# Moving two start-up dependencies in a fused dynamic-convolution and FFN kernel: when w_out is let in, and when w_in's exchanged copies are made

## The chip, the cores and the metric

The kernel runs on one core of one Trainium2 chip. The metric is the device time of one execution in microseconds (us). A *profile* is one execution under the hardware profiler. Its times count from the first instruction, and its span is some 1.7 us shorter than the device time.

## The reference

```python
def _attn_ref(x, weight_gen):              # x (8, 4096, 192), weight_gen (8, 4096, 8, 7)
    w = softmax(weight_gen, axis=-1)       # over the 7 taps
    x_pad = pad 6 zero rows in front of each sequence
    # out[s, head] = sum over k of w[s, head, k] * x_pad[s + k, head]
def _moe_ref(x, w_in, w_out):              # 32768 tokens, w_in (192, 2048), w_out (2048, 192)
    h = np.maximum(x @ w_in, 0.0)
    return h * h @ w_out
```

## The kernel before

The engines are PE (matrix products; PEld is its weight load), DVE (vector work), ACT (activations and copies), GpSimd (POOL in the profile) and SP, which here only issues DMA transfers. The profile infers from the recorded updates of *semaphores* what ended an engine's wait. For each of GpSimd's row DMAs (below) the trace records 16 such updates, its *landings*. I say that a DMA *lands* when its last update is recorded. The *granted clock* is the share of PE's full clock that the profile shows.

The tokens are worked in blocks: two of 512 tokens (one sub-block each), then blocks of 1024 (two sub-blocks). For the third and fourth blocks, where this change acts, DVE makes the softmax weights in pieces, DMAs of up to 16 KB each move their rows to the partitions where they are needed (`wr`; I call these the *row DMAs*), and DVE multiplies the rows by a mask into *bands* (`bd`). PE convolves x with the bands (`yp`), 16 *units* of h matmuls follow, ACT applies relu (`t`), DVE squares (`g`), and the output matmuls (`o`) come in quarters. I call the bands by sub-block: B2 belongs to the third block, B4 to the fourth.

The parts that the change touches, with cuts marked:

```python
    def cross_w_in(q):            # w_i[:, q, 1] is w_i[:, q, 0] with partition halves exchanged
        for r0, r1 in ((0, RT), (RT, 0)):
            nc.sync.dma_start(out=w_i[r0 : r0 + RT, q, 1], in_=w_i[r1 : r1 + RT, q, 0])
    ...
        x_load_f32(0)
        load_w_in(w_st[0], 0, nc.sync)         # first half of w_in, f32 staging
        load_w_in(w_st[1], 1, nc.sync)         # second half
        ...
        x_load_f32(1)                          # second x load, x_st[1]
        s1.load(nc.sync)
        ...
        nc.gpsimd.tensor_copy(out=gate, in_=x_st[1][:, 0:1])   # the gate
        for q in range(4):
            load_w_out(q, 4)                   # on GpSimd, behind the gate
        s2.load(nc.gpsimd)
        x_load(2)
    ...
        plans = {
            0: "B1 X1 W u u u u E1 C S1 u u M u u",
            1: "L3 u u B2 M E2 B3 u M E2 u u S2 u M u C u S2 M",
            2: "L4 u u u E3 M u u u M B4 u u u u M B5 S3 u u u u M u E3 C u",
            ...
        }
    ...
        for j in range(NBLK):
            if j + 2 < NBLK:
                load_rows(j + 2)
            if 1 <= j <= WQ:                   # WQ = 2
                cross_w_in(j - 1)
            u = 0
            for step in plans[j].split():
                ...
```

In a plan `u` is a unit, `M` a quarter of the output matmuls, `C` the next block's convolution, `B` bands, `E` exponentials, `S` a softmax piece, `W` the cast of w_in's second half, `L` a load of weight_gen, `X` a cast of x. The last piece of a small softmax also issues its row DMAs, in turn from SP and from GpSimd. Units 8 to 15 of a paired block need the second exchanged copy of w_in. The gate copy has no result that anyone uses: it makes GpSimd's stream wait for the tile that it reads (5.88 us of idle time ahead of the copy at 14.56 in before). Its intent is to keep w_out from competing with loads needed earlier.

The softmax here doesn't subtract the row's maximum and nothing guards it: scores larger than these inputs give would overflow.

## Time and profile before

| | before |
|---|---|
| device time, median of 3 runs | 739.93 us (739.14 to 740.39) |
| span in the profile | 737.6 us |
| mean granted PE clock | 0.998 |
| PE waits for w_out, once | 1.73 us |
| PE waits for w_in's second exchanged copy, twice | 2.04 and 0.40 us |

The totals of the profile of before give, for each engine, busy microseconds, share of the span and instructions:

```profile
PE 727.1 (99%) x14053; PEld 528.2 (72%) x14053; DVE 630.1 (85%) x858; ACT 613.3 (83%) x731; POOL 97.7 (13%) x139
```

A kernel at 99% PE can be helped only in the few places where PE idles or runs at a lower clock. The timeline of SP's queue of before (start, duration, queue and line, transfer and count) shows why the second exchanged copy is late:

```profile
27.23 1.85 SPq L142 DMA_DIRECT2D w_i<-w_i  x2
...
34.38 10.16 SPq L352 DMA_DIRECT2D wr<-v_first  x6
44.59 2.26 SPq L142 DMA_DIRECT2D w_i<-w_i  x2
```

SP issued these in program order. The second pair of exchanges stands behind six row DMAs, which wait for a softmax piece that ends at 41.33 and are all issued only by 44.54, although the pair's source was ready since 18.23.

### The profile page before, as it was taken

The numbers are of one execution on the slowest core, as the hardware profiler recorded it, in microseconds if no ns is written. First come the engines' busy times: TensorE is split into PE (matmuls) and PEld (weight loads), VectorE is DVE, ScalarE is ACT, GpSimd is POOL, SyncE is SP. The second block draws the span as 40 slices with busy tenths as digits, with TensorE's granted clock in tenths as the row PEclk, the third lists the DMA queues.
The fourth block names the chain that finished last, engine by engine and source line by source line (L and its number), as shares of the span: only waits on it lengthen the run. The fifth ranks groups of instructions, "written<-read, shape, count | busy, mean of one in ns | idle before, by whom it ended". The sixth has DMA issues, their size and how long they took to land.

```text
span 737.6 us, 31011 instructions
## 1 busy us (share of the span) xinstructions
PE 727.1 (99%) x14053; PEld 528.2 (72%) x14053; DVE 630.1 (85%) x858; ACT 613.3 (83%) x731; POOL 97.7 (13%) x139
## 2 busy tenths in 40 slices
PE   8989999999999999999999999999999999999998
PEld 4547778777777777777777777777777777777777
DVE  7988999898899888889888889888889888778853
ACT  5869888888888888888888888888888888888883
POOL 5322221521101100011000110010100110001000
PEclk9999999999999999999999999999999999999999
DMA  7955343966443534454524554425544415444012
GB/s 188 163 86 131 60 74 88 167 137 146 80 87 65 126 94 84 67 136 86 94 56 85 115 123 76 66 58 134 103 86 77 65 49 120 65 86 77 29 44 67
DMA packets 126048, 68.94 MB, mean 93 GB/s; under 512 B 84681, under 2 KB 122012, under 8 KB 125404
## 3 DMA queue, kind: packets, MB, share of 16 engines
q1 hardware_dynamic: 80636, 48.47, 23.2%
q0 software_dynamic: 45136, 18.39, 21.7%
q8 instruction: 110, 1.80, 1.0%
q14 instruction: 22, 0.18, 0.1%
q10 hardware_dynamic: 144, 0.10, 0.0%
HBM read 50.18 MB, written 28.70 MB: 107 GB/s over the span
## 4 chain that ended last, share of the span: by engine, by line
PE 93%; DVE 3%; DMA 1%; ACT 1%; issue 1%; SPq 1%; POOL 0%; DVEq 0%
PE o L614 45%; PE h L565 43%; PE yp L486 4%; DVE g L583 1%; PE yp L520 1%; DVE v_first L261 1%; DVE bd L392 1%; DMA wr<-v_first 0%; DMA wg<-in_weight_gen_dram 0%; DMA w_i<-w_i 0%; DVE ssum L246 0%; DVE rcp L253 0%; SPq L352 0%; POOL wr L352 0%; SPq L142 0%
## 5 line engine op out<-in xcount | busy, mean ns | idle before, releaser
L579 ACT ACTIVATE t<-h 128x1024 f16<-128x1024 f32 x512 | 496.6, 1026 | 64.7 <-PE h L565 61.0
L614 PEld LDWEIGHTS <-g 64*128 64x128 f16 (+1 forms) x8032 | 344.9, 94 | 57.6 <-issue 4.0
L614 PE MATMUL o<-w_o,g 64*128 64x192 f16 (+1 forms) x8032 | 381.1, 243 | 2.1 <-DMA w_o<-in_moe_w_out_dram 1.7
L583 DVE TENSOR_TENSOR g<-t 128x2048 f16<-128x2048 f16 (+1 forms) x309 | 309.6, 1037 | 31.9 <-ACT t L579 31.6
L565 PE MATMUL h<-y,w_p 64*128 64x512 f16 x2400 | 291.7, 376 | 0.0
L565 PEld LDWEIGHTS <-w_p 64*128 64x128 f16 x2400 | 113.9, 94 | 94.7
L392 DVE TENSOR_TENSOR bd<-wr,mask 128x4160 f16<-128x4160 f16 (+3 forms) x89 | 149.4, 1702 | 1.3 <-ACT wr L378 0.7
L630 DVE TENSOR_TENSOR o_sb<-o,o_sb 128x384 f32<-128x384 f32 x123 | 68.4, 556 | 61.3 <-ACT o_sb L628 58.9
L322 POOL DMA_DIRECT2D xt<-in_x_dram x62 | 51.7, 837 | 427.3 <-PE yp L486 341.2
L628 ACT COPY o_sb<-o 128x384 f32<-128x384 f32 x129 | 61.7, 478 | 48.0 <-PE o L614 47.1
L565 PE MATMUL h<-y,w_i 64*128 64x512 f16 x576 | 71.3, 377 | 2.6 <-DMA w_i<-w_i 2.4
L565 PEld LDWEIGHTS <-w_i 64*128 64x128 f16 x576 | 29.6, 94 | 26.2 <-DMA w_i<-w_i 3.2
L486 PEld LDWEIGHTS <-xt 128*32 128x32 f16 x2000 | 24.4, 95 | 10.6 <-issue 10.6
L261 DVE TENSOR_TENSOR v_big<-ex,rcp 128x112 f16<-128x112 f32 (+5 forms) x180 | 29.8, 236 | 1.6 <-DMA vd<-v_big 0.6
L496 DVE CAST y<-yp 128x1024 f16<-128x1024 f32 x25 | 30.4, 1217 | 0.0
L486 PE MATMUL yp<-bd,xt 128*32 128x104 f16 (+1 forms) x2000 | 28.3, 209 | 0.0
L239 ACT ACTIVATE ex<-wg 128x560 f32<-128x560 f32 (+4 forms) x38 | 25.8, 680 | 1.8 <-DMA wg<-in_weight_gen_dram 1.8
L246 DVE TENSOR_REDUCE ssum<-ex 128x80 f32<-128x560 f32 (+4 forms) x38 | 25.3, 666 | 1.2 <-ACT ex L239 1.2
L496 ACT CAST y<-yp 128x1024 f16<-128x1024 f32 x25 | 25.2, 1006 | 0.0
L253 DVE RECIPROCAL rcp<-ssum 128x80 f32<-128x80 f32 (+4 forms) x38 | 22.8, 600 | 1.3
L312 POOL DMA_DIRECT2D xt<-in_x_dram x7 | 3.9, 554 | 125.5 <-PE yp L486 98.8
L352 POOL DMA_DIRECT2D wr<-v_first x24 | 13.0, 567 | 12.5 <-DVE v_first L261 8.7
(40 smaller groups left out, 116.5 us busy)
## 6 DMA issues: line engine op xcount, KB each, us to landing
out_dram<-o_sb SPq DMA_DIRECT2D x63, 384.0 KB
xt<-in_x_dram POOLq DMA_DIRECT2D x42, 240.0 KB, 4.8
wg<-in_weight_gen_dram SPq DMA_DIRECT2D x4, 1064.0 KB
xt<-in_x_dram POOLq DMA_DIRECT2D x20, 192.0 KB, 4.7
wr<-vd SPq DMA_DIRECT2D x38, 80.0 KB
vd<-v_big SPq DMA_DIRECT2D x5, 512.0 KB
y<-y SPq DMA_DIRECT2D x100, 24.0 KB
wg<-in_weight_gen_dram SPq DMA_DIRECT2D x5, 392.0 KB
```

What stands on the lines that cost most here:

```text
L239: nc.scalar.activation(out=self.ex[:, lo:hi].rearrange("p r g k e -> p (r g) k e"), in_=self.wg[:, lo:hi].rearrange("p r (g e) k -> p (r g ...
L261: eng.tensor_tensor(out=bass.AP(tensor=v.tensor, offset=v.offset + lo * H * SL + lo % SL * 2 + g * SL * 2, ap=[list(v.ap[0]), [H * SL + 2, ...
L322: eng.dma_start(out=dst[:, first:last], in_=ap)
L392: nc.vector.tensor_tensor(out=bd_t[j][:, H * lo : H * (lo + len(tiles) * n)].rearrange("p (g m c) -> p g m c", g=shape[1], c=2 * SL), in0= ...
L486: nc.tensor.matmul(out=yp[p0 : p0 + 32, k - k0, a:b], lhsT=x_t[s][:, i, c0 : c0 + 32], rhs=bd[:, head // 2, e, 0 : b - a], start=True, sto ...
L496: copy(out=y[:, k0 : k0 + 2], in_=yp)
L565: nc.tensor.matmul(out=h[:, half], lhsT=w_in_chunk(w, u, slot, half), rhs=y_t[j][r0 : r0 + RT, k], start=(slot == 0), stop=(slot == NK - 1 ...
L579: nc.scalar.activation(out=t1[:, e], in_=h, func=ActF.Relu)
L583: nc.vector.tensor_tensor(out=g[:, a : e + 1], in0=t1[:, a : e + 1], in1=t1[:, a : e + 1], op=AluOp.mult)
L614: nc.tensor.matmul(out=oo[:, cc * Dm : (cc + 1) * Dm], lhsT=g[r0 : r0 + n, cc * P : (cc + 1) * P], rhs=w_o[r0 : r0 + n, fc, :], start=(fc ...
L628: nc.scalar.copy(out=o_sb, in_=o[0][:, c])
L630: nc.vector.tensor_tensor(out=o_sb, in0=o[1][:, c], in1=o_sb, op=AluOp.add)
```

## The change

Its intent is to take away both PE waits. The gate reads a tile that lands earlier, so w_out starts earlier. Both exchanged copies are issued at the head of the second block, ahead of the row moves.

```diff
-        nc.gpsimd.tensor_copy(out=gate, in_=x_st[1][:, 0:1])
+        nc.gpsimd.tensor_copy(out=gate, in_=w_st[1][:, 0:1])
...
-            if 1 <= j <= WQ:
-                cross_w_in(j - 1)
+            if j == 1:
+                for q in range(WQ):
+                    cross_w_in(q)
```

## The prediction

> **What bounds the kernel now.** I read the totals first: PE (TensorE) is busy for 99% of the span, DVE 85%, ACT 83%, and the chain that ended last is 93% PE. So the change can gain only where PE idles or runs slowly. Busy times by stretch put that at the start: PE is busy 53.3 us of the first 60, 59.5 of the next 60 and all 180 of the next 180. The waits from 12 to 60 us name the places:
>
> ```profile
> POOL gate L718 <- DMA x_st<-in_x_dram: 5.9, 1, 5.9
> ...
> PEld L565 <- DMA w_i<-w_i: 3.2, 2, 2.5
> ...
> PE h L565 <- DMA w_i<-w_i: 2.4, 2, 2.0
> ...
> PE o L614 <- DMA w_o<-in_moe_w_out_dram: 1.7, 1, 1.7
> ```
>
> PE waits once for w_out (1.7 us) and twice for the second exchanged copy of w_in (2.0 and 0.4 us). The first goes back to the gate copy on POOL, which waits for the second x load. The timeline of all engines from 0 to 75 us (start, duration, instruction, idle before) shows the order:
>
> ```profile
> 13.93 2.35 DVE L392 TENSOR_TENSOR bd<-wr,mask 128x3328 f16<-128x3328 f16 x2
> ...
> 14.56 1.29 POOL L718 COPY gate<-x_st 128x1 f32<-128x1 f32 x1 [5.88 <-DMA x_st<-in_x_dram]
> ...
> 15.80 3.48 POOL L183 DMA_DIRECT2D w_o<-in_moe_w_out_dram  x4
> ...
> 21.87 1.31 PE L614 MATMUL o<-w_o,g 128*128 128x192 f16 x14 [1.73 <-DMA w_o<-in_moe_w_out_dram]
> ...
> 29.00 4.60 DVE L392 TENSOR_TENSOR bd<-wr,mask 128x4160 f16<-128x4160 f16 x3 [0.52 <-DMA wr<-v_first]
> ```
>
> The matmul timeline from 45 us shows the second wait, and what follows it:
>
> ```profile
> 44.70 1.69 PE L565 MATMUL h<-y,w_i 64*128 64x512 f16 x14
> 48.43 0.39 PE L565 MATMUL h<-y,w_i 64*128 64x512 f16 x1 [2.04 <-DMA w_i<-w_i]
> 49.22 1.58 PE L565 MATMUL h<-y,w_i 64*128 64x512 f16 x9 [0.40 <-DMA w_i<-w_i]
> 50.73 2.74 PE L614 MATMUL o<-w_o,g 128*128 128x192 f16 x16
> 53.41 2.76 PE L565 MATMUL h<-y,w_i 64*128 64x512 f16 x24
> ```
>
> Sixteen output matmuls take 2.74 us here and 1.48 us at 36.34. The half-microsecond stretches (PE, PEld, DVE, ACT, POOL busy, then PEclk) tell why: the granted clock is 0.50 from 50.0 to about 53.4 us.
>
> ```profile
> 49.50:50.00 0.50, 0.50 (x8) 0.23 (x5) 0.00 (x0) 0.15 (x1) 0.00 (x0) 1.00 0.71 282
> 50.00:50.50 0.50, 0.50 (x5) 0.00 (x0) 0.00 (x0) 0.50 (x1) 0.00 (x0) 0.50 0.20 82
> ...
> 53.00:53.50 0.50, 0.50 (x5) 0.20 (x5) 0.50 (x1) 0.00 (x0) 0.00 (x0) 0.59 0.00 0
> 53.50:54.00 0.50, 0.50 (x6) 0.21 (x6) 0.50 (x1) 0.48 (x1) 0.00 (x0) 1.00 0.00 0
> ```
>
> [...] a gap from 46.4 to 48.4, then 3.4 us at 0.50; the shorter gap from 20.1 to 21.9 left the clock at 1.00. [...] the one-element gate copy takes 1.29 us and ends at 15.85, just as the first of the two band products ends (15.73). [...]
>
> **The change, part by part.** The instruction orders of both kernels have equal lengths but for one merged row; nothing is added. Two things move.
>
> *1. The gate.* It now waits for the 512 KB load of w_st[1]. That load is the sixth of SP's first transfers; 2.2 MB lie up to its end, which DMA's running total reaches at about 10.2 us. Other loads finished 1 to 1.5 us behind that total (x_st[0] on ACT at 6.91), so I take 11.3 us. DVE's band products end at 11.57, so the copy should be done by 12, and the w_out issues begin near 11.8 instead of 15.80: 4 us earlier. The chunk that PE waited for lands at about 17.9 instead of 21.87. PE wants it at 20.1, so the wait of 1.73 us goes. w_out's bytes start about 1.6 us after the issue (15.80 to 17.4 in the DMA share), so near 13.4, while the second x load landed at 14.5. Only its tail, and one 392 KB weight_gen load, then share the engines. x has slack: DVE casts it at 16.20, after the band products, and ACT needs weight_gen at 18.13.
>
> How much of 1.73 us survives? DVE has no idle time from 13.3 to 25.7, so the second softmax still ends at 23.90. Its rows go through DMA (wr) to the bands that start at 29.00 and end at 33.60, and the third block's convolution follows at 34.07. PE moved by 1.73 would be there at 32.3. The bands gain where DVE waited: three products at 25.95, 26.86 and 27.78 waited for ACT, which waited 2.15 us for PE. Back to back they end near 27.6. The rows' landing then binds: GpSimd's wr take 3.5 us beside a DMA that is over 100% busy up to 27 us, and 2.4 us in the quieter stretch from 41 to 46. With w_out, weight_gen and x out of the way by 24 us they gain about 1 us. So the bands start at 28.0 and end at 32.6. **First part: 1.3 us** (0.5 to 1.7).
>
> *2. The exchange.* Its second pair moves from 44.59, behind six wr issues that waited for the softmax, to right behind the first pair. That one takes 1.85 us from 27.23, so the second is issued from 29.1 to 31 and lands by 34, against 49.2. PE's need at 46 is met. It waits behind no new semaphore: w_in's second half was converted at 18.2. SP's next load slips from 29.19 to 31, needed at 41.4.
>
> From 44.70 to the convolution at 58.07 PE issues 24 h matmuls, 16 o, 24 h, 32 o, 6 h. At full clock those take 2.72 (24 h at 63.95), 1.32 (start to start of 16 o at 31.90), 2.72, 1.32 and 0.65: 8.7 us, so it would be there at 53.4. It loses 4.65 us: 2.8 in the two waits with their restarts, 1.85 at half clock. DVE's work from 45.59 to its bands' end is 2.3 + 4 x 0.65 + 2.3 = 7.2 us, so they are ready at 52.8: no limit. ACT's from 45.57 is 1.94 + 2.01 + 0.48 + 4.93 + 0.51 + 1.50 = 11.4 us, so y is done at 56.9 against 61.0. PE's next h matmuls need that y. ACT binds, and **the second part is 4.1 us** (3.0 to 4.6).
>
> Sum 5.4 us. After 60 us PE lost 0.5 us of 60 and then nothing, so an early shift is kept to the end. ACT will not run wholly without waits, for which I take off 0.4: 5.0 us, 739.9 to **734.9 us**.
>
> **Rivals.** (a) *Exchange hidden, w_out gain lost.* The softmax to wr to bands path is DVE's and does not start earlier. If the rows land no sooner, the convolution stays at about 33.6 and part 1 gives 0.4: 735.8. For it: DVE without idle time. Against: the busy DMA of 20 to 27 us empties sooner.
> (b) *w_out collides with x.* If x landed after 16.2 us, DVE's whole chain would slip by the excess; each us is lost until about 34 us. With 1 us late, 736.5. For it: DMA is full from 8 to 14 us. Against: the slack of 1.7 us and the late start of w_out's bytes.
> (c) *DVE takes over.* After 45.6 us its idle time up to 62 is only 1.80 + 0.29 + 2.03 = 4.1 us. If g lags, the gain of part 2 falls to 2.5 or 3: 736 to 736.5. Against: its consumers come about half a block later.
> (d) *Only the wait goes and the slow clock stays.* If the slow spell is not the gap's, part 2 is 2.3 us: 736.5. Against: the 3.4 us spell directly behind the longest gap.
>
> **Range and chances.** Everything full and ACT unhindered: 733.4. A single rival: 736 to 736.5, and the runs before spread over 1.25 us. So 733.3 to 737.0. A change over 2% needs 14.8 us, three times everything in reach, and no part can cost nearly that: within 2% has 0.98, faster 0.015, slower 0.005.
>
> **What would show it.** Right: no PE wait for w_o near 20 us; gate copy near 11.5 and w_o issues near 12; no wait for w_i; granted clock 1.00 in every stretch from 44 to 60 us; third block's convolution near 32.7 and the fourth's (58.07 before) near 53. Wrong: the cast of x or the second softmax later than 16.2 and 23.9; the wr landing still at 29; ACT idle between 45 and 57 us; a slow clock elsewhere[...].

## The result, and the profile after

| | before | after |
|---|---|---|
| device time, median of 6 runs | 739.39 us (738.29 to 740.39) | 735.86 us (735.24 to 737.04) |
| ratio | | 0.9954, 95% interval 0.9941 to 0.9967 |
| span in the profile | 737.6 us | 733.6 us |
| mean granted PE clock | 0.998 | 1.000 |

A ratio here is the mean time of one kernel's runs over that of the other's of the same rounds, so it is not quite the ratio of the medians. The kernel is 3.5 us faster by the medians: within 2%, and inside the predicted range.

**The gate.** The timeline of POOL, then two rows of PE's, of the kernel after (start, duration, engine, line, instruction, count, and in brackets the idle time ahead and what ended it):

```profile
13.10 0.18 POOL L718 COPY gate<-w_st 128x1 f32<-128x1 f32 x1 [4.42 <-DMA w_st<-in_moe_w_in_dram]
13.23 3.14 POOL L183 DMA_DIRECT2D w_o<-in_moe_w_out_dram  x4
...
19.88 1.48 PE L614 MATMUL o<-w_o,g 128*128 128x192 f16 x16
...
32.24 2.12 PE L520 MATMUL yp<-bd,xt 128*32 128x104 f16 x120
```

The copy takes 0.18 us here, with DVE idle, where it took 1.29 beside a band product in before (14.56 to 15.85, the product 13.93 to 15.81). w_out is issued 2.57 us earlier than before (13.23 against 15.80). The chunk that PE had waited for landed at 18.68 instead of 21.82, and PE's first 16 output matmuls run without a break. The third block's convolution starts at 32.24 instead of 34.07. Behind it PE is 1.27 us ahead of before, but that is this execution: in a second profile of the same kernel (e3 below) it is 0.37.

**The exchange.** The timeline of SP's queue after:

```profile
27.57 2.46 SPq L142 DMA_DIRECT2D w_i<-w_i  x4
...
32.56 12.75 SPq L352 DMA_DIRECT2D wr<-v_first  x6
```

All four exchanges are issued by 30.03. PE's timeline after, in the stretch where before had its waits and its half clock, and one half-microsecond stretch (busy PE, PEld, DVE, ACT, POOL, then PEclk):

```profile
46.15 1.49 PE L614 MATMUL o<-w_o,g 128*128 128x192 f16 x16
47.58 2.76 PE L565 MATMUL h<-y,w_i 64*128 64x512 f16 x24
50.18 1.48 PE L614 MATMUL o<-w_o,g 64*128 64x192 f16 x32
51.50 0.81 PE L565 MATMUL h<-y,w_i 64*128 64x512 f16 x6
...
52.92 1.84 PE L520 MATMUL yp<-bd,xt 128*32 128x104 f16 x118 [0.46 <-DVE bd L392]
...
58.98 0.34 PE L614 MATMUL o<-w_o,g 64*128 64x192 f16 x4 [0.19 <-DVE g L583]
...
62.90 1.33 PE L614 MATMUL o<-w_o,g 64*128 64x192 f16 x28 [0.91 <-DVE o_sb L630]
```

```profile
50.00:50.50 0.50, 0.50 (x12) 0.38 (x10) 0.50 (x2) 0.50 (x2) 0.00 (x0) 1.00 1.01 324
```

The waits for w_i are gone, sixteen output matmuls take 1.49 us instead of 2.74, and the clock is 1.00. The six h matmuls ahead of the fourth block's convolution start at 51.50; in before they start at 57.33. So PE is 5.83 us ahead here. But then come three waits that before did not have, all on DVE: 0.46, 0.19 and 0.91 us, 1.56 in sum. The span ends 4.0 us earlier, not 5.8.

DVE's timeline after shows where it fell behind, at the bands B2 and B4; B4 in before comes first:

```profile
45.59 2.32 DVE L392 TENSOR_TENSOR bd<-wr,mask 128x4160 f16<-128x4160 f16 x1
```

```profile
28.33 2.33 DVE L392 TENSOR_TENSOR bd<-wr,mask 128x4160 f16<-128x4160 f16 x1 [1.00 <-issue]
...
44.08 0.69 DVE L583 TENSOR_TENSOR g<-t 128x1024 f16<-128x1024 f16 x1 [0.22 <-ACT t L579]
46.33 2.32 DVE L392 TENSOR_TENSOR bd<-wr,mask 128x4160 f16<-128x4160 f16 x1 [1.56 <-PE h L565]
```

In before, DVE did B4 at 45.59 with no idle time. After the change, with all of PE's work ahead, DVE idles 1.56 us and does B4 *later*, at 46.33. From there DVE runs without a break until past PE's last new wait, so what it owes PE stays late. The releaser that the profile names, an h matmul, is not what DVE needed. The semaphores show it: of GpSimd's five row DMAs B4 needs the first three, and the third lands last. It was issued at 42.42. By 44.20, 15 of its 16 landings were in; the last came at 46.06, and DVE started 0.27 us after that. So the last landing came 1.86 us behind the other fifteen, and DVE started only after it.

B2 was held in what looks like the same way. In every kernel of this document it starts 0.17 or 0.18 us after the last landing of GpSimd's third row DMA. In the kernel after, 15 of the 16 were in by 27.10 and the last at 28.16; in e3 they were in by 27.93 and 29.05. So how much of the gate's lead survives B2 changes from one execution to the next.

What held that last landing? The DMA view of the kernel after, narrowed to 43.25 to 43.50 us, has a packet of another queue (queue, kind: packets, MB, share of 16 engines; and below, transfer, count, KB, median us from issue to landing):

```profile
q8 instruction: 1, 0.02, 37.8%
...
wr<-v_first POOLq DMA_DIRECT2D x2, 16.0 KB, 3.3
```

It is a 16 KB packet of kind "instruction", started at 43.36, that took 1.51 us. Another ran from 26.14 to 27.06, beside B2's rows. There are 110 of these in the execution, 1.80 MB. I take them to be PE's own instruction stream; the profile gives their kind but not whose instructions they are. What speaks for it is that the packet near 43 us keeps step with PE: eight kernels have the same PE instructions up to there (the first six of the table below, f1 and f4), and in seven of them exactly 1190 PE and PEld records of the trace start before it (1208 in f1). The trace does not say which of the 16 DMA engines carried it, so at this point the link was only a theory.

### The profile page after: what moved, and what is told of

Its sections match the earlier page's. It is cut to its first block, busy times and chain, and to the rows that moved or that the text cites.

```text
span 733.6 us, 31012 instructions
## 1 busy us (share of the span) xinstructions
PE 726.4 (99%) x14053; PEld 528.5 (72%) x14053; DVE 628.7 (86%) x858; ACT 613.1 (84%) x731; POOL 97.0 (13%) x139
## 4 chain that ended last, share of the span: by engine, by line
PE 92%; DVE 5%; DMA 1%; issue 1%; ACT 0%; POOL 0%; DVEq 0%
PE o L614 45%; PE h L565 42%; PE yp L486 4%; DVE g L583 2%; DVE bd L392 1%; PE wp L679 1%; DMA wr<-v_first 1%; PE yp L520 1%; DVE v_first L261 1%; POOL wr L352 0%; DVE rcp L253 0%; DVE ssum L246 0%; ACT w_i L713 0%; PE pr L369 0%; DVE w_i L881 0%
## 5 line engine op out<-in xcount | busy, mean ns | idle before, releaser
L352 POOL DMA_DIRECT2D wr<-v_first x24 | 13.0, 565 | 15.8 <-DVE v_first L261 11.3
```

## The experiments

Every kernel below gave a correct result, and each was timed in 5 rounds beside before on the same chip. Three chips were used, so medians are compared within a batch (e, f, g) and ratios across batches. Before had medians of 739.08, 739.10 and 740.06 us in the three batches.

### Which part of the change carries the gain?

**e1_gate_only**: before, with the new gate alone.

```diff
-        nc.gpsimd.tensor_copy(out=gate, in_=x_st[1][:, 0:1])
+        nc.gpsimd.tensor_copy(out=gate, in_=w_st[1][:, 0:1])
```

> Only the gate moves; the second exchange stays behind the softmax rows. Theory (the gate's gain is kept only as far as the DVE chain softmax, rows, bands moves, and the exchange follows that chain): no w_out wait near 20 us, third block's convolution 1.3 us earlier, but the exchanged copy still lands near 48.5, PE idles about 2.6 us and the clock falls to 0.50 for 3.4 us, mean granted clock 0.998; total gain 0.4 to 0.9 us, near 738.7. Rival (the gate is worth its full 1.3 us or more by itself): gain 1.3 to 1.7 us.

Measured: 739.54 us (738.52 to 741.37), ratio 1.0004 (0.9989 to 1.0018). The gate alone is worth nothing that these runs resolve. The interval ends at a gain of 0.8 us, so it leaves room for the lower part of what I expected, but not for the rival's 1.3. The wait for w_out is gone and the third block's convolution starts at 32.25, as in the kernel after; behind it PE is 0.84 us ahead of before. Then comes a longer wait for the second exchanged copy, which still stands behind SP's row DMAs. PE's wait for the copy (us in total, times, longest), and B4 in DVE's timeline:

```profile
PE h L565 <- DMA w_i<-w_i: 2.8, 2, 2.4
```

```profile
46.25 2.33 DVE L392 TENSOR_TENSOR bd<-wr,mask 128x4160 f16<-128x4160 f16 x1 [1.07 <-DMA wr<-v_first]
```

The copy's last landing is at 48.73 against 49.17 in before, so PE, which came 0.84 us earlier, waits 2.45 and 0.39 us, and the fourth block's convolution starts at 57.66 against 58.07: 0.41 us is left. B4 is 0.66 us later than in before, again behind a late row DMA, and the profile names it here; but between it and the convolution PE has no wait for DVE, so no loss shows here. The record shows one thing more: in three of the six runs the mean clock is 0.995, as in one of the 31 runs of before in these batches. These three average 740.4 us, the other three 738.8. So the longer gap may have cost more clock in some runs; no such run has a kept profile, and that stays open.

**e2_exchange_only**: the kernel after, with the old gate.

```diff
-        nc.gpsimd.tensor_copy(out=gate, in_=w_st[1][:, 0:1])
+        nc.gpsimd.tensor_copy(out=gate, in_=x_st[1][:, 0:1])
```

> Only the exchange moves; the gate still waits for the second x load. Theory (after 46 us DVE bounds the stretch, and its start is the landing of the fifth sub-block's rows, which the gate moves little): no w_in wait, clock 1.00 throughout, w_out wait of 1.7 us still there, PE ahead of DVE by 1 us less so it waits less for DVE; gain 3.3 to 4 us, that is nearly all of the whole change. Rival (the parts add up, 1.3 for the gate): gain 2.2 to 2.7 us.

Measured: 735.01 us (734.12 to 738.12), ratio 0.9946 (0.9928 to 0.9965): 4.0 us, the whole gain. The profile of this kernel shows PE's waits, 12 to 64 us (what waited, for what: us in total, times, longest):

```profile
PE o L614 <- DVE o_sb L630: 0.9, 1, 0.9
PE o L614 <- DMA w_o<-in_moe_w_out_dram: 0.7, 1, 0.7
```

The wait for w_out is there again. Against e3, the same kernel with the new gate, it cost nothing in these profiles: PE's lead over before behind the third block's convolution is 0.45 us here and 0.37 in e3, behind the fourth's 4.17 and 4.16, and the DVE wait (0.9) is in both. In e3 the gate's lead was gone by then: B2 started at 29.22 behind a late row DMA (29.14 here). B4's idle time is 1.41 us here, and its releaser is `DMA wr<-v_first`.

**e3_after_again**: the kernel after, unchanged, to see whether DVE's lateness is one profile's accident.

```diff
(no edit)
```

> The changed kernel once more, to see what of its trace repeats. If DVE takes over regularly: bands of the fifth sub-block start 1 us or more after DVE is free, PE waits for bands near 52 us and for the output sum near 62 us, gain 3.3 to 4.0 us. If the late rows were chance: bands start as soon as DVE is free (near 44.8), no PE wait for the output sum, profiled run 1 us faster than before.

Measured: 735.87 us (735.37 to 736.18), ratio 0.9953 (0.9941 to 0.9964). B4 idles 1.36 us behind the row DMA, and PE waits 0.91 for the output sum. The lateness is regular. What does not repeat is the gate's lead behind the third block's convolution, 0.37 us against 1.27. The intervals of e2 and e3 overlap, so the two cannot be told apart.

### Does the gap trip the clock?

**e4_gap_filled**: before, with nine dummy matmuls where PE waits for the exchanged copy. Their result is overwritten by the unit that follows.

```diff
     def st_unit(j, u):
         h = ps_h.tile([P, 2, TB], f32, name="h", tag="h")
+        if j == 2 and u == 8:
+            for _ in range(9):
+                nc.tensor.matmul(
+                    out=h[:, 0], lhsT=warm[:, 0:P], rhs=warm, start=True, stop=True,
+                    skip_group_check=True,
+                )
```

> The kernel before with nine full-size idle matmuls (128x512, 1.94 us) ahead of unit 8 of the third block, in the gap in which PE waits for the exchanged copy; their result is overwritten. Theory (the gap trips the clock): the wait for the copy ends as before near 49 us, but the clock stays 1.00, sixteen output matmuls take 1.48 us and not 2.74, gain 1.5 to 1.9 us. Rival (the slow spell comes from something else): clock 0.50 again, no gain or a loss.

Measured: 737.14 us (736.53 to 738.10), ratio 0.9971 (0.9959 to 0.9984), 2.1 us faster by the ratio, although PE still cannot start its useful work before the copy has landed. PE's timeline of this kernel:

```profile
46.13 2.12 PE L561 MATMUL h<-warm 128*128 128x512 f16 x9
48.18 1.66 PE L571 MATMUL h<-y,w_i 64*128 64x512 f16 x12
49.78 1.49 PE L620 MATMUL o<-w_o,g 128*128 128x192 f16 x16
...
55.86 1.57 PE L520 MATMUL yp<-bd,xt 128*32 128x104 f16 x120
```

The sixteen output matmuls take 1.49 us against 2.74 in before, the clock is 1.00 in every stretch from 44 to 60 us, and the convolution starts 2.2 us earlier (55.86 against 58.07). Of these 2.2 us some 0.6 are chance, since the second copy's last landing came at 48.55 in this execution and at 49.17 in before's; that leaves 1.6 us for the clock. So in these profiles it is the idle gap, not the stretch of work, that brings the half clock: 0.50 from 50.00 to 53.41 us in before, behind idle times of 2.04 and 0.40 us, and 1.00 here with the gap filled. How long a gap it takes is not shown; before's idle time of 1.73 us ahead of 21.87 left the clock at 1.00. Nor do all runs of before lose clock. Of the 31 runs of before in the three batches, 25 have a mean clock of 0.998 or less and average 739.6 us, and six have 0.999 or 1.000 and average 737.7, which is 1.9 us less. The exchange's 4.0 us are thus 1.6 to 2.1 for the clock, and the rest for the wait.

### Where did the rest go?

**f1_s2_together**: the kernel after, with the last softmax piece ahead of B4 made directly behind the one before it, so that its rows are issued about 1.7 us earlier.

```diff
-            1: "L3 u u B2 M E2 B3 u M E2 u u S2 u M u C u S2 M",
+            1: "L3 u u B2 M E2 B3 u M E2 u u S2 S2 u M u C u M",
```

> The changed kernel with the second piece of the third softmax moved up next to its first piece (three units earlier on DVE), so the rows of the fifth sub-block are issued about 1.9 us earlier. Theory (DVE's idle 1.4 to 1.6 us before that sub-block's bands is a wait for the rows' last sixteenth, and it is this that makes DVE late for the output sum): rows land by 45, bands start when DVE is free near 44.8, the PE waits for bands (0.3 to 0.5 us) and for the output sum (0.9 us) go, 1.0 to 1.5 us faster than the changed kernel, near 734.6. Rival (DVE's work after 46 us is simply too much): bands no earlier in effect, same time as the changed kernel within 0.3 us.

Measured: 733.88 us (733.52 to 734.19), ratio 0.9931 (0.9915 to 0.9947). GpSimd's third row DMA lands at 42.49. B4 starts without idle time, and PE's wait for the output sum is gone:

```profile
44.59 2.32 DVE L392 TENSOR_TENSOR bd<-wr,mask 128x4160 f16<-128x4160 f16 x1
```

The instruction packet comes at 44.28, when all rows are in.

**f4_s2_old_gate**: f1 with the old gate.

```diff
-        nc.gpsimd.tensor_copy(out=gate, in_=w_st[1][:, 0:1])
+        nc.gpsimd.tensor_copy(out=gate, in_=x_st[1][:, 0:1])
```

> The same reordering with the old gate: exchange moved, softmax pieces together, gate on the second x load. Theory (once the rows no longer bind, the gate's gain on PE, w_out wait of 0.7 to 1.7 us, is kept in part): 0.4 to 1.2 us slower than the reordered kernel with the new gate. Rival (the gate is worth nothing in any case, because the third block's convolution waits for its own rows in both): equal within 0.4 us.

Measured: 735.19 us (734.33 to 735.69), ratio 0.9949 (0.9934 to 0.9964). Against f1 on the same chip that is 1.3 us slower, and the ranges do not overlap. So once rows no longer hold B4, the new gate is 1.3 us faster in time, as much as the prediction gave it. That the wait for w_out is what costs f4 this is not shown: the profiled run was f4's fastest, with the gate copy already at 13.81 and no such wait.

**f5_more_pe_instr**: the kernel after, with 21 warm-up matmuls turned into 13 of the same size and 36 small ones. PE has 28 matmuls more, 56 instructions with their weight loads, ahead of the real work, so that its instruction packets fall elsewhere.

```diff
+        def tiny(n):
+            for i in range(n):
+                nc.tensor.matmul(
+                    out=wp[:, 0:64], lhsT=warm[:, 0:P], rhs=warm[:, 0:64], start=True, stop=True
+                )
...
-        spin(21)
+        tiny(24)
+        spin(13)
+        tiny(12)
```

> The changed kernel with the 21 warm-up matmuls made into 13 full and 36 small ones: 56 more PE instructions before the work, same warm-up time. Theory (the rows' last sixteenth is late because a 16 KB instruction-fetch packet, [...] falls on them; the fetch follows PE's instruction count, so it comes 1 to 2 us earlier): fetch near 41.5 to 42.4 and not 43.4 to 44.2, the third rows transfer lands within 0.3 us of its other fifteen sixteenths, bands start near 45, 1.0 to 1.5 us faster than the changed kernel, near 734.6. Rival (rows late for another reason[...]): fetch moves, the late sixteenth stays, no gain.

Measured: 732.96 us (731.98 to 733.29), ratio 0.9917 (0.9902 to 0.9932), the fastest of all. Against the kernel after that is about 2.7 us (0.9953 less 0.9917, times 739), more than I expected. Its packet came at 40.17, before the rows were issued, and DVE's timeline shows

```profile
43.61 0.69 DVE L583 TENSOR_TENSOR g<-t 128x1024 f16<-128x1024 f16 x1 [0.22 <-ACT t L579]
44.22 2.32 DVE L392 TENSOR_TENSOR bd<-wr,mask 128x4160 f16<-128x4160 f16 x1
```

B4 follows the squares with no idle time, 2.1 us earlier than after. PE's wait for the output sum shrinks from 0.91 to 0.17, and those for bands and g are gone. The third row DMA's fifteenth landing is at 43.82 and its sixteenth at 43.88, so the rival, which foretold a late sixteenth in any case, is refuted. B2 came earlier too (27.86 against 28.33). In the two profiles f5 is 0.46 us ahead of the kernel after behind the third block's convolution, 1.4 behind the fourth's and 2.1 at 67 us, so the larger part arises behind B4.

**f3_no_gate**: the kernel after without any gate, to test the prediction's rival (b), that early w_out collides with x.

```diff
-        nc.gpsimd.tensor_copy(out=gate, in_=w_st[1][:, 0:1])
```

> The changed kernel without a gate: w_out is issued as soon as GpSimd has cleared its buffer, near 8.7 us, amid the loads of w_in and x. Theory [...]: w_in's and x's loads land 1 to 3 us later, the cast of x on DVE starts after 17.5 us instead of 16.5, everything behind slips, 0.8 to 2.5 us slower than the changed kernel. Rival (SP's loads come first anyway or have slack): within 0.4 us of the changed kernel.

Measured: 735.49 us (734.85 to 736.09), ratio 0.9953 (0.9939 to 0.9968), as with the gate. w_out is issued at 8.61 and the cast of the second x still comes at 16.31, against 16.54 with the gate: no collision. My expectation of one was wrong. Why before needed a gate at all, this does not tell.

### Controls

**g1_both**: f1 and f5 together (both diffs). Both are supposed to cure the same loss, so they should not add.

```diff
-        spin(21)
+        tiny(24)
+        spin(13)
+        tiny(12)
...
-            1: "L3 u u B2 M E2 B3 u M E2 u u S2 u M u C u S2 M",
+            1: "L3 u u B2 M E2 B3 u M E2 u u S2 S2 u M u C u M",
```

> The changed kernel with the 56 further PE instructions and the third softmax's pieces together. Theory (both remove the same loss, the wait of the fifth sub-block's bands for its rows): no more than 0.4 us faster than the better of the two alone, 732.6 to 733.3. Rival (they remove different losses): 1 us faster than either, near 732.0 or less.

Measured: 733.08 us (732.57 to 733.89), ratio 0.9913 (0.9892 to 0.9933): no better than f5 alone by the ratios, and 0.35 us from g4, which has f5's kind of edit, on the same chip. The two cure the same loss.

**g2_old_gate_more_instr**: e2 with f5's warm-up.

```diff
-        nc.gpsimd.tensor_copy(out=gate, in_=w_st[1][:, 0:1])
+        nc.gpsimd.tensor_copy(out=gate, in_=x_st[1][:, 0:1])
...
-        spin(21)
+        tiny(24)
+        spin(13)
+        tiny(12)
```

> The exchange alone (old gate) with the 56 further PE instructions. Theory (the gate is worth the w_out wait once rows do not land late): 0.8 to 1.5 us slower than the changed kernel with the same instructions (732.96), near 734.0. Rival (the gate is worth nothing whatever the fetch does): equal within 0.4 us.

Measured: 736.07 us (735.13 to 736.88), ratio 0.9953 (0.9932 to 0.9975), so 2.6 us slower than g4 and 3.0 slower than g1 on the same chip, more than I expected of the gate. The profile shows the rest. With the old gate a packet falls at 27.79, beside B2's rows, and DVE waits there:

```profile
30.73 4.13 DVE L392 TENSOR_TENSOR bd<-wr,mask 128x4160 f16<-128x4160 f16 x2 [2.40 <-DMA wr<-v_first]
```

All five of GpSimd's row DMAs, of which B2 needs three, land late here, at 30.01 to 31.42. Two causes are mixed in this kernel, so it gives no clean value of the gate; f1 against f4 does.

**g3_before_more_instr**: before with f5's warm-up, to see whether the small matmuls help by themselves.

```diff
-        spin(21)
+        tiny(24)
+        spin(13)
+        tiny(12)
```

> Control: the kernel before with the 56 further PE instructions. Theory (they help only where a fetch falls on rows that bind; in the kernel before PE waits for the exchanged copy and the slow clock follows): within 0.7 us of the kernel before, clock 0.998 as before. Rival (the small matmuls themselves make the start faster): 2 to 3 us faster, as in the changed kernel.

Measured: 738.82 us (737.13 to 739.48), ratio 0.9984 (0.9963 to 1.0004). The interval holds 1, so they do not help in a way that these runs resolve; it reaches down to a gain of 2.7 us, so time alone does not exclude the rival's 2. The profile speaks against it: PE is 0.6 us behind before after the third block's convolution, and the span is only 0.3 us shorter.

**g4_fewer_more_instr**: the kernel after with only 20 instructions more.

```diff
-        spin(21)
+        tiny(8)
+        spin(17)
+        tiny(6)
```

> The changed kernel with 14 small matmuls for 4 full ones: 20 further PE instructions and not 56, the fetch only 0.4 to 0.8 us earlier, near 42.7 to 43.6, so still on the rows of the fifth sub-block. Theory: its third rows transfer has a late sixteenth again, bands wait 0.8 us or more, time within 0.6 us of the changed kernel, 735.3 to 736.2. Rival (any small warm-up matmuls help): 1 us or more faster, near 734.5 or less.

Measured: 733.43 us (733.10 to 734.42), ratio 0.9919 (0.9898 to 0.9939), nearly as good as f5. I had expected the packet to move by less than a microsecond and the rows to be late again. It moved from 43.36 to 41.29, and B4 was not held (44.24). That packets move in proportion to the instructions put ahead of them is thus not shown, and why they moved so far is open; by the trace's PE records it came 32 of the kernel's own instructions earlier, not 20 (in f5 50, not 56). The theory that a packet beside the rows holds B4 survives, because it predicts from the packet's time, whatever set it.

### The packet and the rows, over ten kernels

From the traces: the instruction packet near 43 us, the landing of the last row DMA that B4 needs from GpSimd, and B4 itself. In the first five the packet ends while that DMA is still under way.

| kernel | packet, start to end | rows landed | B4 starts | DVE idle before it |
|---|---|---|---|---|
| after | 43.36 to 44.87 | 46.06 | 46.33 | 1.56 |
| e1, gate only | 43.73 to 44.74 | 45.98 | 46.25 | 1.07 |
| e2, exchange only | 44.24 to 45.55 | 46.73 | 47.01 | 1.41 |
| e3, after again | 44.20 to 45.50 | 46.75 | 47.03 | 1.36 |
| f3, no gate | 43.48 to 44.42 | 45.67 | 45.94 | 0.99 |
| before | 44.59 to 45.82 | 44.86 | 45.59 | none |
| e4, gap filled | 44.84 to 46.07 | 44.59 | 45.62 | none |
| f1, softmax together | 44.28 to 45.38 | 42.49 | 44.59 | none |
| f5, more instructions | 40.17 to 41.50 | 43.88 | 44.22 | none |
| g4, fewer more | 41.29 to 42.31 | 43.97 | 44.24 | 0.05 |

In all of the first five the rows' last landing comes 1.2 to 1.3 us after the packet's end, and B4 0.27 or 0.28 us after the landing. B4 was not held where the packet came after the rows or nearly so (before, e4, f1), nor where it came early enough (f5, g4). In g4 it did delay the first of these row DMAs, to 43.50, again 1.2 us after its end, but the third was in at 43.97, in time. Before shows the same effect harmlessly: its packet at 44.59 delayed the fourth and fifth of GpSimd's row DMAs to 47.00 and 47.16, which B4 does not need. The other four fit too, with no idle time before B4: in f4 the packet (43.69 to 45.26) came after the landing (42.62); in g2 and g3 it had ended (43.82 and 43.50) before that DMA was issued (44.83 and 44.26); in g1 (40.62 to 41.83) it delayed all five, the third to 43.45, still before B4 at 44.50. At B2 the last landing in the kernel after, e1, e3, f1 and f3 is 1.07 to 1.18 us behind the end of its packet, too. That the packet is the cause is well supported by moving it (f5, g4) and by moving the rows (f1). That they share a DMA engine is not shown, since the trace does not name engines.

The table also says why the change ran into it. Against before, the kernel after has the packet 1.23 us earlier, since it kept step with PE (1190 records ahead of it in both), but the third row DMA was issued only 0.68 us earlier (42.42 against 43.10), since it follows DVE's softmax. What was a margin became an overlap.

## Why the prediction was right, and where a term was not

- **Total.** 734.9 was predicted and 735.86 measured; the range of 733.3 to 737.0 holds it. The gain was 3.5 us by the medians where the sum said 5.0.
- **Gate, on PE.** The mechanism held. The copy came at 13.10, not 11.3 to 12, so w_out was 2.6 us earlier and not 4: the load it waits for, SP's seventh and not its sixth, landed at 13.05 where 11.3 was reckoned (before's own trace has it at 12.16). That was enough: the chunk landed at 18.68 and PE wanted it at 19.88. PE came out of the third block's convolution 1.27 us earlier, as predicted: the next h matmuls start at 34.30 against 35.57. That the size fits is partly luck. B2's bands were predicted at 28.0 and came at 28.33, but not by the reckoned path: the rows, but for one landing of the third row DMA, came 1.45 us earlier than before (27.10 against 28.55), and that last landing, 1.10 us after a packet's end, came only 0.66 earlier. In e3 the same kernel has a lead of 0.37.
- **Gate, in time.** In this order of work the gate brought nothing to the end that the runs resolve (e1: ratio 1.0004; e2 without it as fast as e3 with it). Where B4 isn't held, f1 is 1.3 us faster than f4. So the size fits, but not what the end kept of it.
- **Exchange.** Right in mechanism: 4.1 us predicted, 4.0 alone (e2, interval 2.6 to 5.3), of which 1.6 to 2.1 is the clock where 1.85 was reckoned (e4, which refutes rival (d)). That the sizes agree so well is partly luck, since e2 has DVE waits of 1.4 us that the prediction did not count. The gap ahead of the slow clock was 2.04 us and then 0.40; that such a gap halves the clock as a rule is not shown. At 51.50 us PE is 5.8 us ahead, a little more than the sum of 5.4.
- **The failed term.** It is the deduction: "ACT will not run wholly without waits, for which I take off 0.4". PE's three new waits, 1.56 us in sum, are on DVE. The step behind it, "so they are ready at 52.8: no limit", counted DVE's work from 45.59 as back to back and took the rows' landing as given. B4 started at 46.33 because a row DMA's last landing came at 46.06. "ACT binds" held only up to y: ACT's chain began at 44.30 and y was done at 55.84, 11.5 us later where 11.4 was reckoned, with one wait of 0.56 us for the convolution, which itself waited for bands. From B4 on PE's waits are all on DVE and none on ACT.
- **Rivals.** (c) happened, in a smaller size than the 2.5 or 3 us it would have left of part 2, and for a reason that the prediction lacked. (b) is refuted by f3. (a) did not happen in the profile of after, where the third block's convolution came 1.8 us earlier; but in e3, the same kernel, the rows' last landing was no sooner (29.05 against 28.82 in before) and the gate gave 0.37 us on PE, close to the 0.4 that (a) foretold. There, too, a packet had ended 1.18 us before that landing, so the packet, and not DVE alone, is the likely cause.
- **The time shift of the end.** 5.83 less 1.56 is 4.3, and the spans differ by 4.0. Comparing PE's matmuls one by one, after is 4.9 us ahead behind the fourth block's convolution, which its bands slow by more than the 0.46 us of idle time, 3.8 ahead at 67 us, and 4.0 from 108 us on. So nearly all is lost in this stretch and little changes behind it.

## What to carry to other kernels

When a wait is taken off the busiest engine, ask of every other stream whether it moves by the same amount; here the instruction packet, in step with PE, moved by 1.2 us and the rows by 0.7, and a landing that used to be in time was not. Small transfers with a consumer close behind deserve a margin: issuing them three units earlier (f1; 1.7 us) gave some 1.6 us more than the change itself (ratio 0.9931 against 0.9953). And a gap that looks like 2.4 us on PE cost 4 here, so check the granted clock behind it before you size its removal.
